# Sliding-window attention beside a gated FFN, forward and backward: the short FFN chunk as one block, U's rows turned from SBUF, and fillers on PE

## The chip, the cores and the metric

The kernel runs on one NeuronCore of a Trainium2 chip. The metric is the device time of one execution in microseconds (us). The engines are named as in the profile: PE (TensorE, with PEld for its weight loads), DVE (VectorE), ACT (ScalarE), POOL (GpSimd) and SP (SyncE), which here only issues transfers. "Queue" means the order of an engine's instructions, which is fixed when the program is built.

## The reference

Inputs are x (2048 x 512), the attention weights wqkv and wo, the FFN weights W_gate, W_up (512 x 1376) and W_down (1376 x 512), a gate vector and grad_out, all bf16. Computed are the output and the gradients of x and of all weights (eight tensors):

```python
def _A_ref(x, wqkv, wo):                       # 32 heads of 16, window of 256 keys
    q, k, v = ...                              # x @ wqkv, split into heads
    scores = jnp.einsum("bhqd,bhkd->bhqk", q, k) * (Dh ** -0.5)
    scores = jnp.where(mask, scores, -1e9)     # 0 <= query - key < 256
    return heads_joined(softmax(scores) @ v) @ wo

def _B_ref(x, W_gate, W_up, W_down):           # 1376 columns: ten chunks of 128 and one of 96
    gate = x @ W_gate
    return ((gate * (gate > 0)) * (x @ W_up)) @ W_down

g = sigmoid((x * gate_w).sum(-1, keepdims=True))
out = g * _A_ref(x, ...) + (1 - g) * _B_ref(x, ...)
# and the vector-Jacobian product of out with grad_out
```

## The kernel before

**A planner fixes the order.** The kernel describes its work as operations with costs in ns, ranks, and the buffers that they read and write (`Flow.op`, L210). `Flow.run` (L257) then plays the work through on a model of the five engines, one event after another, and emits each instruction at the moment at which the model starts it. On an engine it takes the ready operation of the lowest rank, and among equal ranks the one described first. A transfer on SP has a cost for its issue (430 ns, 1300 ns for a turning one, if nothing else is given) and a model of the DMA engines for its end. So the costs, ranks and buffer counts set the order of every queue; the chip then runs those queues as they are. PE work is of three modes ("row" for scores, "col" for sums over keys, "den" for dense 128 x 128 matmuls), and a change of mode costs 98 ns in the model. The eight PSUM banks are shared by kinds of work, each with a cap (`bank`).

**The stages.** First, to some 55 us, the inputs are loaded, turned to column form, and the first quarter of the projections is made. Then attention runs over 32 stages (`NS`; eight groups of four heads times four blocks of 512 rows, one U per stage). Its "row" operations have rank 0; all dense work has higher ranks and fills what PE has left: projections of the other head groups (`proj`, rank 3.5, L715), `front(fc)` of the FFN chunks (rank 4, L803), `back(fc)` (rank 4, L850), the weight gradients `dw(c)` of attention (4.05 to 4.7, L1190) and the FFN products for the first twelve row tiles (`early`, 4.6). After attention, from about 730 us, come the last row tiles, `final` and `whole`, and dw(3).

**The FFN around the change.** `front(fc)` makes, for each of four blocks of 512 rows, three products (L828) of a chunk's 128 columns, and stores them to DRAM as `ffn_d[fc, w, p, s]` (L830). Chunk 10 has only 96 columns (`fsz`). `back(fc)` needs the same data with rows in the partitions: `load_acts` turns them with DMA transposes, one per block for a full chunk (L840, three products at once, 384 rows) and three per block for the short one (L845, 96 rows each). `back` then makes 16 matmuls into each of five banks (L855 on, by way of `accumulate`, whose matmuls are recorded at L622) and stores three results. The loop over chunks (L1102) goes 0 to 10, `back` three chunks behind `front` (`LAG`), and the last three `back`s stand at the end. `group(g)` (L1238) reads the FFN products of all chunks again (L1245, L1248, L1253) for the dense products that are recorded at L1300; its transfers depend on all of `ffn_d`, so none can start before the last chunk is stored.

**U.** In each stage `tasks_A1` (L1021) computes U (128 x 512), which DVE and POOL use. The key-side sums (`tasks_N`, matmuls at L1012) need U with rows in the partitions, R. U is stored to DRAM (`U_d[n]`, L1049) and read back by a DMA transpose (L1050). U has one buffer, R three.

**Other lines in the numbers.** L944: row matmuls; L986: exponentials on ACT; L992: DVE products of attention; L962: masks on POOL; L889 to L891: loads of a stage; L1070 and L1093: stores of attention's results `HD_d`; L1194: turns of `HD_d` for dw; L1276: loads of `HD_d` for the tail.

Of the kernel before, what the change touches and what calls it, by code (L numbers as in the profile page):

```python
# [44 lines left out]
PE, DVE, ACTE, POOL, SP = "PE", "DVE", "ACT", "POOL", "SP"  # L45
LATENCY = {PE: 230, DVE: 130, ACTE: 150, POOL: 100, SP: 2300}
SWITCH = 98
BACKLOG = 1500
HOLD, WAIT = 2.5, 800

# [148 lines left out]
class Flow:  # L199
# [7 lines left out]
    def __init__(self):  # L207
        self.ops = []
# [48 lines left out]
    def run(self):  # L257
# [4 lines left out]
        self.log = []  # L262
# [6 lines left out]
        def offer(o):  # L269
            o.at = now  # L270
            for e in o.times:
                ready[e].append(o)

# [9 lines left out]
        while done < len(self.ops):  # L283
            progress = True
            while progress:
                progress = False
                for e in (PE, ACTE, DVE, POOL, SP):
# [3 lines left out]
                    if dma_free > now + BACKLOG:  # L291
                        cands = [o for o in cands if o.rank < 3 or not o.nbytes]
                    if not cands:
                        continue
# [12 lines left out]
                    if e == PE:  # L307
                        if o.mode != mode:
                            took += SWITCH
                        mode = o.mode  # L310
                        if o.mode == "den":
                            heavy = o.heavy
# [20 lines left out]
            while events and events[0][0] <= now:  # L333
                _, _, what, o = heapq.heappop(events)
                if what == "done":
                    done += 1
                    o.state = 2
                    if not o.lead:
                        for b in o.uses:
                            b.drop()  # L340
                    release(o.after)
                elif what == "lead":
                    for b in o.uses:
                        b.drop()
# [3 lines left out]
def kernel(  # L348
# [61 lines left out]
    ffn_d = Buf(None, dram.tile([FC, 3, P, S], BF, name="ffn_d"))  # L410
    U_d = [Buf(None, dram.tile([P, W], BF, name=f"U_d{n}")) for n in range(NS)]
# [391 lines left out]
    def front(fc):  # L803
        fs = fsz(fc)
        wg, wu, wdT = wsets.pop(("f", fc))
        for tg in range(NSB):
# [20 lines left out]
            for k, (a, b) in enumerate((("rg", "upm"), ("dhs", "upm"), ("dhs", "rg"))):  # L827
                op({POOL: t_pool(W, 2), DVE: DTT}, lambda e, q=q, k=k, a=a, b=b: EN[e].tensor_tensor(  # L828
                    out=q["act"][:fs, k, :], in0=q[a][:fs, :], in1=q[b][:fs, :], op=ALU.mult), r=[q[a], q[b]], w=[(q["act"], k)], rank=3)
            dma(lambda q=q, sl=sl: nc.sync.dma_start(ffn_d[fc, :, :fs, sl].rearrange("w p s -> p w s"), q["act"][:fs]), r=[q["act"]],  # L830
                w=[(ffn_d, (fc, tg))], nbytes=384 * KB, rank=2)

    def load_acts(fc):
        fs = fsz(fc)
        rows = []
        for tg in range(NSB):
            sl = slice(tg * W, (tg + 1) * W)
            rw = buf("rows")
            if fs == P:
                dma(lambda rw=rw, sl=sl: nc.sync.dma_start_transpose(  # L840
                    out=rw[:].rearrange("p k w f -> p k (w f)"), in_=ffn_d[fc, :, :, sl].rearrange("w p s -> (w p) s")),
                    r=[(ffn_d, (fc, tg))], w=[rw], nbytes=384 * KB, rank=2, turn=True, ns=1500)
            else:
                for w in range(3):
                    dma(lambda rw=rw, sl=sl, w=w: nc.sync.dma_start_transpose(out=rw[:, :, w, :fs], in_=ffn_d[fc, w, :fs, sl]),  # L845
                        r=[(ffn_d, (fc, tg))], w=[rw], nbytes=100 * KB, rank=2, turn=True)
            rows.append(rw)
        return rows

    def back(fc):  # L850
        rows = load_acts(fc)
        fs, f0 = fsz(fc), fc * P
        wst, dst = buf("wst"), buf("dst")
        for c in range(DC):
            bank = buf("mm")  # L855
            accumulate(bank, [mm(lambda bank=bank: bank[:, 0:2 * fs], lambda t=t, c=c: x_r[:, t, c * P:(c + 1) * P],
                                 lambda t=t: rows[t // 4][:, t % 4, 1:3, :fs]) for t in range(NT)], rows + [x_r], BACK, [wst],
                       cols=2 * fs, step=8)
            op(either(2 * P), lambda e, bank=bank, c=c: copy(e, wst[:, c, :, :fs],
                                                             bank[:, 0:2 * fs].rearrange("p (a f) -> p a f", a=2)),  # L860
               r=[bank], w=[wst], rank=2)
# [4 lines left out]
        accumulate(bank, [mm(lambda: bank[:fs, :D], lambda t=t: rows[t // 4][:, t % 4, 0, :fs], lambda t=t: db_r[:, t, :])  # L866
# [154 lines left out]
    def tasks_A1(n, us):  # L1021
# [10 lines left out]
        def b1(segs):  # L1032
# [16 lines left out]
        dma(lambda: nc.sync.dma_start(U_d[n][:], U[:]), r=[U], w=[U_d[n]], nbytes=128 * KB, rank=1)  # L1049
        dma(lambda: nc.sync.dma_start_transpose(out=R[:], in_=U_d[n][:]), r=[U_d[n]],  # L1050
            w=[R], nbytes=128 * KB, rank=1, turn=True)
# [50 lines left out]
    for fc in range(FC):  # L1102
        if fc:
            load_ffn(fc)
        front(fc)
        if fc >= LAG:
            back(fc - LAG)
    for fc in range(FC - LAG, FC):
# [129 lines left out]
    def group(g):  # L1238
# [3 lines left out]
        for f in range(0, FC, 4):  # L1242
# [4 lines left out]
            if f + 4 > NF:  # L1247
                dma(lambda gh=gh, hi=hi, f=f: nc.sync.dma_start(gh[:fl_, hi - f, :], ffn_d[hi, 0, 0:fl_, gsl]), r=[ffn_d], w=[gh],  # L1248
                    nbytes=48 * KB, rank=3.1)
            hs.append(gh)  # L1250
        for f in range(FC):
            gd = buf("gd")
            dma(lambda gd=gd, f=f: nc.sync.dma_start(gd[:fsz(f)], ffn_d[f, 1:3, :fsz(f), gsl].rearrange("w p s -> p w s")),  # L1253
                r=[ffn_d], w=[gd], nbytes=128 * KB, rank=3.1, row=512)
# [198 lines left out]
    with tc.manual_schedule(engines={eng.PE, eng.Activation, eng.DVE, eng.Pool, eng.SP}):  # L1453
        fl.run()
# [27 lines left out]
```

## Time and profile before

| | before |
|---|---|
| three runs | 849.79, 860.8, 861.84 us |
| median | 860.8 us |
| profiled execution: span, first to last instruction | 853.1 us |
| profiled execution: its own end-to-end time | not listed; the median is 7.7 us above its span |
| mean granted TensorE clock | 0.984 |
| PE busy | 810.4 us (95%) |
| DVE busy | 707.9 us (83%) |
| ACT busy | 598.6 us (70%) |
| POOL busy | 526.6 us (62%) |
| DMA packets, bytes | 317818, 156.38 MB |

The profile is of one execution. Its page has busy times, the span in 40 slices of 21.3 us (each digit a tenth of busy time, or of the granted clock), DMA queues, the chain of waits that ended last, and the costliest groups of instructions. Asked for stretches, it gives for each engine busy us and, in parentheses, the number of instructions, then the granted PE clock, the DMA share and GB/s. Matmuls are pipelined and their records overlap, so a busy PE is not PE at its peak. SP's rows (SPq) are issues: their length is the time that the issue held the queue, not that of the transfer.

### The profile page before, as it was taken

The numbers are of one execution on the slowest core, as the hardware profiler recorded it, in microseconds if no ns is written. First come the engines' busy times: TensorE is split into PE (matmuls) and PEld (weight loads), VectorE is DVE, ScalarE is ACT, GpSimd is POOL, SyncE is SP. The second block draws the span as 40 slices with busy tenths as digits, with TensorE's granted clock in tenths as the row PEclk, the third lists the DMA queues.
The fourth block names the chain that finished last, engine by engine and source line by source line (L and its number), as shares of the span: only waits on it lengthen the run. The fifth ranks groups of instructions, "written<-read, shape, count | busy, mean of one in ns | idle before, by whom it ended". The sixth has DMA issues, their size and how long they took to land.

```text
span 853.1 us, 24192 instructions
## 1 busy us (share of the span) xinstructions
PE 810.4 (95%) x8834; PEld 388.9 (46%) x8952; DVE 707.9 (83%) x1312; ACT 598.6 (70%) x1212; POOL 526.6 (62%) x928
## 2 busy tenths in 40 slices
PE   8999999999999999999999989899999999899996
PEld 5534533535354544544545445443333435343444
DVE  3579899999999999998999998898999899614333
ACT  4778888888888778777888878888887787100113
POOL 5469778676697887777987755656665655002111
PEclk9999999999999999999999969999999999899999
DMA  7989656465699999899555367968655643768793
GB/s 204 230 179 224 165 147 184 119 149 142 135 239 226 214 219 218 238 206 207 152 132 117 90 159 184 279 157 242 197 174 152 179 150 101 220 186 281 214 221 99
DMA packets 317818, 156.38 MB, mean 183 GB/s; under 512 B 202817, under 2 KB 310402, under 8 KB 316930
## 3 DMA queue, kind: packets, MB, share of 16 engines
q1 hardware_dynamic: 302522, 141.78, 66.7%
q10 hardware_dynamic: 14600, 11.47, 4.5%
q0 software_dynamic: 576, 1.57, 1.0%
q8 instruction: 70, 1.15, 0.6%
q14 instruction: 50, 0.41, 0.2%
HBM read 55.02 MB, written 59.93 MB: 135 GB/s over the span
## 4 chain that ended last, share of the span: by engine, by line
PE 48%; DMA 10%; DVE 5%; issue 3%; ACT 2%; POOL 1%; SPq 1%; ACTq 1%; DVEq 0%; POOLq 0%
PE banks L622 16%; PE banks L1300 11%; PE banks L944 9%; DMA arena<-HD_d 7%; PE banks L1012 6%; DVE arena L992 3%; PE banks L1215 3%; PE banks L1213 2%; ACT arena L986 1%; DMA arena<-ffn_d 1%; SPq L1194 1%; PE banks L1045 1%; DMA arena<-QD_d_1_119 1%; DMA arena<-U_d_76 1%; DMA arena<-dx_p_145 1%
## 5 line engine op out<-in xcount | busy, mean ns | idle before, releaser
L992 DVE TENSOR_TENSOR arena<-arena,banks 128x512 bf16<-128x512 bf16 (+2 forms) x768 | 460.0, 646 | 33.5 <-PE banks L944 19.9
L986 ACT ACTIVATE arena<-banks 128x512 bf16<-128x512 f32 (+2 forms) x768 | 398.5, 573 | 81.5 <-PE banks L944 72.3
L962 POOL TENSOR_SCALAR_AFFINE_SELECT arena<-arena 128x256 bf16<-128x256 bf16 (+1 forms) x736 | 350.3, 499 | 168.0 <-ACT arena L986 150.3
L622 PE MATMUL banks<-arena 128*128 128x512 bf16 (+3 forms) x1648 | 333.9, 335 | 9.6 <-issue 2.9
L622 PEld LDWEIGHTS <-arena 128*128 128x128 bf16 (+1 forms) x1728 | 151.6, 99 | 138.3 <-issue 55.9
L1300 PE MATMUL banks<-arena 128*128 128x512 bf16 (+1 forms) x747 | 184.2, 384 | 5.4 <-issue 2.1
L944 PE MATMUL banks<-arena 32*128 32x384 bf16 (+2 forms) x2816 | 165.6, 278 | 10.1 <-DVE arena L992 3.0
L944 PEld LDWEIGHTS <-arena 32*128 32x128 bf16 x2816 | 51.2, 92 | 149.6 <-issue 137.1
L600 ACT CAST arena<-banks 128x512 bf16<-128x512 f32 (+4 forms) x173 | 84.1, 497 | 47.4 <-PE banks L622 24.4
L1300 PEld LDWEIGHTS <-arena 128*128 128x128 bf16 (+1 forms) x784 | 70.0, 98 | 94.9 <-issue 21.5
L828 POOL TENSOR_TENSOR arena<-arena 128x512 bf16<-128x512 bf16 (+1 forms) x87 | 102.0, 1174 | 16.8 <-DVE arena L823 11.3
L1012 PE MATMUL banks<-arena 128*32 128x384 bf16 (+5 forms) x2816 | 103.6, 280 | 4.3 <-DVE arena L992 1.6
L1012 PEld LDWEIGHTS <-arena 128*32 128x32 bf16 (+1 forms) x2816 | 58.8, 95 | 42.3 <-issue 25.2
L1397 POOL TENSOR_TENSOR arena<-arena 128x512 f32<-128x512 f32 x12 | 15.2, 1266 | 100.0 <-DMA arena<-dx_p_143 45.6
L1213 PE MATMUL banks<-arena 128*128 128x128 bf16 x256 | 45.5, 221 | 3.3 <-DMA arena<-HD_d 3.1
L1041 POOL TENSOR_TENSOR arena<-arena 128x512 bf16<-128x512 f32 x32 | 37.3, 1166 | 17.7 <-ACT arena L1038 8.6
L1396 ACT ACTIVATE arena<-gw_b,arena 128x512 f32<-128x512 bf16 x12 | 8.5, 719 | 56.4 <-DMA arena<-HD_d 27.2
L1215 PE MATMUL banks<-arena 128*128 128x256 bf16 x256 | 47.7, 274 | 0.0
L828 DVE TENSOR_TENSOR arena<-arena 128x512 bf16<-128x512 bf16 (+1 forms) x45 | 31.7, 716 | 3.1 <-ACT arena L600 1.7
L823 DVE SCALAR_TENSOR_TENSOR arena<-arena,banks 128x512 bf16<-128x512 bf16 (+1 forms) x44 | 29.9, 680 | 2.8 <-PE banks L622 1.8
L1213 PEld LDWEIGHTS <-arena 128*128 128x128 bf16 x256 | 24.3, 98 | 9.3 <-issue 8.6
L1215 PEld LDWEIGHTS <-arena 128*128 128x128 bf16 x256 | 25.2, 98 | 6.8 <-issue 3.4
(91 smaller groups left out, 482.3 us busy)
## 6 DMA issues: line engine op xcount, KB each, us to landing
ffn_d<-arena SPq DMA_DIRECT2D x40, 384.0 KB
arena<-ffn_d SPq DMA_DIRECT2D x88, 128.0 KB
out_dram<-arena SPq DMA_DIRECT2D x66, 128.0 KB
HD_d<-arena SPq DMA_DIRECT2D x64, 128.0 KB
arena<-ffn_d SPq DMA_DIRECT2D x16, 256.0 KB
arena<-HD_d ACTq DMA_DIRECT2D x24, 128.0 KB
arena<-HD_d ACTq DMA_DIRECT2D x35, 64.0 KB
arena<-HD_d SPq DMA_DIRECT2D x29, 64.0 KB
```

Source lines behind the costliest of these rows:

```text
L600: nc.scalar.copy(out, in_)
L622: return lambda start, stop: nc.tensor.matmul(out_fn(), lhsT=lhs_fn(), rhs=rhs_fn(), start=start, stop=stop)
L828: op({POOL: t_pool(W, 2), DVE: DTT}, lambda e, q=q, k=k, a=a, b=b: EN[e].tensor_tensor(out=q["act"][:fs, k, :], in0=q[a][:fs, :], in1=q[b] ...
L944: nc.tensor.matmul(bank, lhsT=lt[rs, ls], rhs=rt[rs, rsl], start=True, stop=True)
L962: nc.gpsimd.affine_select(out=v.rearrange("p h (b k) -> p h b k", b=cnt), in_=v.rearrange("p h (b k) -> p h b k", b=cnt), compare_op=ALU.i ...
L986: op({ACTE: t_act(w)}, lambda e, h=h: nc.scalar.activation(nxt.Pt[:, h, :w], nxt.S[h][:, :w], ACT.Exp), r=[nxt.S[h]], w=[(nxt.Pt, h)], rank=0)
L992: op({DVE: t_dve(wc)}, lambda e, h=h: nc.vector.tensor_tensor(out=cur.Pd[:, h, :wc], in0=cur.Pt[:, h, :wc], in1=cur.dP[h][:, :wc], op=ALU. ...
L1012: nc.tensor.matmul(acc[32 * i:32 * i + wt.shape[1], q0:q0 + cnt * P], lhsT=wt, rhs=m[:, i % 2, col * P:(col + cnt) * P], start=(k == 0), s ...
L1041: op({POOL: t_pool(W, 2), DVE: t_dve(W)}, lambda e: EN[e].tensor_tensor(out=U[:], in0=ri[:], in1=qd[:], op=ALU.mult), r=[ri, qd], w=[U], r ...
L1213: nc.tensor.matmul(bank[:, 0:P].rearrange("p (g d) -> p g d", d=Dh), lhsT=x_r[:, t, cd * P:(cd + 1) * P], rhs=RW[:, t, 0:2 * P].rearrange( ...
L1215: nc.tensor.matmul(bank[:, P:3 * P], lhsT=x_r[:, t, cd * P:(cd + 1) * P], rhs=RW[:, t, 2 * P:4 * P], start=False, stop=stop, skip_group_ch ...
L1300: nc.tensor.matmul(bank[:], lhsT=l_(), rhs=r_(), start=(lo + k == 0), stop=(lo + k == n - 1))
```

## The change

Five edits go together:

1. The short chunk's products go to a tensor of their own, `ffn_l`, of 3 x 96 rows in one block, and each block of 512 rows is turned by one transfer of 288 rows, so that the short chunk takes 4 turning transfers, not 12. In the turned buffer its three products stand side by side (96 columns each) instead of 128 apart, and `back` reads them there (`row_of`). The readers of the products in `group` follow.
2. The chunks are worked in the order 0, 1, 2, 3, 4, 10, 5, 6, 7, 8, 9.
3. U is no longer stored to DRAM: the DMA transpose reads it from SBUF.
4. Fillers: when the planner has nothing that PE could start, after 20 us of its time, with a PSUM bank free and fewer than 3600 cycles of PE work in its last 3413 ns, it emits a matmul of the identity with 512 columns of x into the free bank, whose result nobody reads. The bank returns to the free ones when the model has the filler done.
5. The planner's model of PE has a clock: windows of 3413.3 ns, and in a window after one with fewer than 3000 cycles of work, PE's operations take twice their cost. Each PE operation of a rank between 3.4 and 4.3 gets a random 0 to 0.02 added to its rank, from a fixed seed.

```diff
+START = 20000
+SEED = 6
+SPAN, LOW, NEED, PHASE = 3413.3, 3000, 3600, 0
...
+        def lately():
+            return sum(b - max(a, now - SPAN) for a, b in self.busy[-40:] if b > now - SPAN) * 2.4
+
+        def ahead(start, took):
+            w, scale = int((start + PHASE) // SPAN), 1
+            if w not in self.slow:
+                self.slow[w] = ran.get(w - 1, 0) < LOW
+            scale = 2 if self.slow[w] else 1
...
+            return took * scale
...
+        rnd = random.Random(SEED)
+        for o in self.ops:
+            if PE in o.times and o.mode != "row" and 3.4 < o.rank < 4.3:
+                o.rank += rnd.uniform(0, 0.02)
...
+                    if e == PE and not cands and self.spare and self.spare.free and lately() < NEED and now > START:
+                        bank = self.spare.free.pop(0)
+                        took = ahead(now + SWITCH * (mode != "den"), 213) + SWITCH * (mode != "den")
+                        mode = "den"
+                        self.fill(bank)
...
                     if e == PE:
+                        took = ahead(now + SWITCH * (o.mode != mode), took)
...
-    ffn_d = Buf(None, dram.tile([FC, 3, P, S], BF, name="ffn_d"))
-    U_d = [Buf(None, dram.tile([P, W], BF, name=f"U_d{n}")) for n in range(NS)]
+    ffn_d = Buf(None, dram.tile([NF, 3, P, S], BF, name="ffn_d"))
+    ffn_l = Buf(None, dram.tile([3 * (F - NF * P), S], BF, name="ffn_l"))
...
-                for w in range(3):
-                    dma(lambda rw=rw, sl=sl, w=w: nc.sync.dma_start_transpose(out=rw[:, :, w, :fs], in_=ffn_d[fc, w, :fs, sl]),
-                        r=[(ffn_d, (fc, tg))], w=[rw], nbytes=100 * KB, rank=2, turn=True)
+                dma(lambda rw=rw, sl=sl: nc.sync.dma_start_transpose(
+                    out=rw[:].rearrange("p k w f -> p k (w f)")[:, :, :3 * fs], in_=ffn_l[:, sl]),
+                    r=[(ffn_l, tg)], w=[rw], nbytes=288 * KB, rank=2, turn=True, ns=1400)
...
+        def row_of(t, lo, hi):
+            return rows[t // 4][:, t % 4].rearrange("p w f -> p (w f)")[:, lo * fs:hi * fs]
...
-        dma(lambda: nc.sync.dma_start(U_d[n][:], U[:]), r=[U], w=[U_d[n]], nbytes=128 * KB, rank=1)
-        dma(lambda: nc.sync.dma_start_transpose(out=R[:], in_=U_d[n][:]), r=[U_d[n]],
-            w=[R], nbytes=128 * KB, rank=1, turn=True)
+        dma(lambda: nc.sync.dma_start_transpose(out=R[:], in_=U[:]), r=[U], w=[R], nbytes=128 * KB, rank=1, turn=True)
...
-    for fc in range(FC):
+    chunks = list(range(5)) + [NF] + list(range(5, NF))
+    for j, fc in enumerate(chunks):
         if fc:
             load_ffn(fc)
         front(fc)
-        if fc >= LAG:
-            back(fc - LAG)
-    for fc in range(FC - LAG, FC):
+        if j >= LAG:
+            back(chunks[j - LAG])
+    for fc in chunks[FC - LAG:]:
         back(fc)
...
+        fl.spare = psum
+        fl.fill = lambda b: nc.tensor.matmul(banks[:, b * W:(b + 1) * W], lhsT=ident[:], rhs=x_r[:, 0, :], start=True, stop=True)
         fl.run()
```

## The prediction

> **What bounds the kernel now.** I read the page's totals first, then busy time by stretch, then the narrow stretches in which the granted clock drops, then the timelines of PE and SyncE around them, then the chain of waits.
>
> ```profile
> span 853.1 us, 24192 instructions
> PE 810.4 (95%) x8834; PEld 388.9 (46%) x8952; DVE 707.9 (83%) x1312; ACT 598.6 (70%) x1212; POOL 526.6 (62%) x928
> PEclk9999999999999999999999969999999999899999
> ```
>
> The PE row is nearly full, but its records overlap in a pipelined engine, so 95% is not yet a bound. The clock row has two dips, at slice 24 and at slice 35. By stretch:
>
> ```profile
> core 0: us, PE busy (x) PEld busy (x) DVE busy (x) ACT busy (x) POOL busy (x), PEclk, DMA share, GB/s
> 55.00:490.00 435.00, 421.38 (x5034) 204.24 (x5105) 412.81 (x726) 356.84 (x715) 343.52 (x578) 1.00 0.76 177
> 490.00:510.00 20.00, 17.79 (x168) 7.63 (x169) 18.66 (x41) 14.18 (x31) 12.07 (x25) 0.66 0.64 161
> 510.00:730.00 220.00, 212.54 (x2648) 97.08 (x2676) 200.47 (x368) 174.10 (x359) 128.46 (x260) 0.99 0.65 180
> 730.00:853.00 123.00, 109.15 (x583) 52.15 (x590) 46.11 (x118) 18.70 (x41) 15.19 (x12) 0.97 0.74 206
> ```
>
> Attention (55 to 730) has two near-full engines: DVE 412.81 + 18.66 + 200.47 = 631.9 of 675 us (94%) and PE. What DVE leaves idle there, 43 us, is the most that better timing can give while its work stays. After 730 DVE is at 37% and PE at 89%: the tail is PE with transfers in between. The hand-over from FFN to the later dense work lies at 490:
>
> ```profile
> 490.00:495.00 5.00, 4.83 (x50) 2.04 (x50) 5.00 (x14) 4.81 (x11) 4.19 (x10) 0.67 0.58 142
> 495.00:500.00 5.00, 3.30 (x44) 1.21 (x40) 5.00 (x13) 4.70 (x12) 3.19 (x7) 0.50 0.39 106
> 500.00:505.00 5.00, 4.67 (x35) 1.54 (x36) 5.00 (x10) 2.35 (x5) 2.67 (x5) 0.50 0.59 152
> 735.00:740.00 5.00, 4.78 (x15) 1.59 (x12) 1.50 (x2) 0.00 (x0) 0.00 (x0) 0.50 0.75 220
> 491.27 0.51 SPq L830 DMA_DIRECT2D ffn_d<-arena  x1
> 491.83 2.50 SPq L845 DMA_TRANSPOSE arena<-ffn_d  x2
> ...
> 496.37 4.72 SPq L845 DMA_TRANSPOSE arena<-ffn_d  x3
> 499.96 0.58 PE L944 MATMUL banks<-arena 32*128 32x256 bf16 x5 [1.68 <-DVE arena L992]
> 501.96 1.49 PE L622 MATMUL banks<-arena 128*128 128x512 bf16 x3 [0.33 <-issue]
> ```
>
> The reader is to see: the short chunk's last store goes out at 491.27, its turns (L845) hold SyncE until 501.1, and PE has no dense matmul (L622) from 487.8 to 501.96. The clock is granted at half meanwhile, and DVE is full all the same. Lastly the places where the chain of waits runs through U's round trip to DRAM:
>
> ```profile
> 354.50 1.95 DMA U_d_72<-arena
> ...
> 445.56 4.67 DMA arena<-U_d_76
> ...
> 535.00 3.38 DMA arena<-U_d_80
> ...
> PE banks L1012 <- DMA arena<-U_d_80: 1.4, 1, 1.4
> PE banks L1012 <- DMA arena<-U_d_76: 0.4, 1, 0.4
> ```
>
> **The base of the sum.** The profiled execution has a span of 853.1 us; its own end-to-end time is not listed. The three runs are 849.79, 860.8 and 861.84; one is shorter than this span, so the profiled execution is like the two longer ones. I take 860.8 - 853.1 = 7.7 us as what lies around the span and sum against 860.8, the median.
>
> **U's rows turned from SBUF.** Removed: 32 stores (L1049, some 0.43 us of SyncE each, 13.7 us) and their landing. The turn stays one instruction (L1050, 1.2 us, 40.9 us in all). Today its issue follows the store's by 4.6 us in the median stage (1.7 to 7.8, from the starts of the two lines), partly behind other issues. SyncE's rows add up to 550 us of 853 (455 of 675 in attention), so the issue time saved lies beside other work except near 490, where SyncE is 90% issued. What can reach the end is R landing some 4 us sooner: at least PE's own 1.8 us of waits, at most the chain's 1.95 + 4.67 + 3.38 = 10.0 us. I take 5, since DVE loses 2.05 of 5 us in 535 to 540 as well. U has one buffer; it is now held until the turn has read it, not the store, so the next U (one per 21 us stage) is not near that limit. No transfer of before turns out of SBUF, so its price is unknown. The nearest rows are DRAM turns: 1.2 us for 128 x 512, up to 5.04 us (L1194, four times the bytes, at 808). At 5.04, SyncE would issue 32 x (5.04 - 1.28 - 0.43) = 107 us more, within its 220 idle us in attention, but each R would come about as late as today: no gain. I take 1.3, the row of the same shape.
>
> **The short chunk: one block, sixth in order.** Twelve turns (15.7 us of SyncE) become four. A full chunk's four (L840) take 1.57 us each in the median, so four of 288 rows cost about 6: 9.7 us less. Moved sixth, everything that this chunk issues moves: three weight loads, four stores, four turns and three result stores on SyncE, and on POOL and DVE its products (1.17 and 0.72 us each). Today the sixth chunk's stores go out at 264 to 292 and its turns three chunks later; SyncE is 77% issued there (154.9 of 200 us in 230 to 430) and the DMA share near 1.0. The cover is that fronts and backs of three chunks overlap; if it is gone, it costs this chunk's turns, 6 us. Last comes a full chunk: after its last store one turn of about 1.6 us and a landing, instead of 10.7 us to the first dense matmul; I put this at 5, so dense work resumes 5.7 us sooner. That is the upper end. The lower is set by the pace of attention, counted in DVE products (L992): 22 in 490 to 510 and 21 in 510 to 530 against 23.1 per 20 us, so 3.2 of 23.1, or 2.8 us. I take 3. The contiguous 2 x 96 columns in back() change no row's size and cost nothing: the same 16 matmuls per bank.
>
> **Fillers and the planner's clock.** They go where the planner has nothing for PE and under 3600 of 8192 cycles of recent work. In the trace this fits the half-clock stretches: by (1 - clock) x length x 2 they are 13.6 us at 490 to 510, 3.4 at 539 to 543 and 6.9 at 733 to 741, 23.9 in all. If all of PE's lost cycles counted, that is 12 us. The lower bound is what the tail alone shows: 15 long matmuls in 735 to 740 against 24 in a full stretch, 9 x 0.21 = 1.9 us. The runs themselves spread by 12.05 us, which is the size of the upper end, so I take 9, nearer to it. A filler costs its 0.21 us in PE's order plus a weight load of 0.1 beside it; PE idles 13.9 us in the tail, which is the cover; without it, 50 fillers would cost 10 us. I take 1 off: clock 8 net.
>
> [...]
>
> **Ranks and order.** The random 0 to 0.02 reorders only first pieces of ranks between 3.4 and 4.3: projections 1 to 3, front() and back(). Projections of the second and third quarter of the heads are stored by 94 and 160, and the second is first loaded at 176, so a swap of the two is hidden; front() is a chain and cannot swap within itself. Bounds: DVE's 43 idle us on one side, and on the other stages like that from 354.5 to 379.3 (24.8 us against 21.3), one or two of which cost 3.5 to 7. Value taken: 0.
>
> Sum: 860.8 - 5 - 3 - 8 = 844.8, so 845. The attention part of it (about 12) fits in DVE's 43.
>
> **The rivals.**
> - The dip stays: 490 to 510 leaves PE 2.2 us idle, room for seven fillers of 0.31 us, and if these do not lift the activity that the clock follows, its term is nil: 860.8 - 8 = 853. For it: long records of waiting matmuls already fill the row. Against: the planner sees rows of 0.3 us where the trace has 26 in 3.62 us, so it sees more room.
> - Hidden anyway: DVE sets the pace and was full through the dip. Only PE's waits for U (1.8) and the tail's 1.9 come back: 857. For it: DVE 5.00 in three rows at half clock. Against: DVE idles 4.3 us in 505 to 530 right after.
> - All ends at once: 10.0 + 5.7 + 12 = 27.7, so 833, with the clock held everywhere. For it: the 849.79 run, with the same program. Against: it needs the upper end three times.
> - Fillers in PE's way: the planner's idle is not PE's idle; in 750 to 830 PE is busy 95%. With 60 fillers at 0.31 us and no gain from the clock: 860.8 - 5 - 3 + 19 = 872; it is slower than before from some 26 fillers on.
> - SBUF turns are dear: SyncE has 220 idle us in attention, or 6.9 per stage; with the 1.71 of today's store and turn, it is full from 8.6 us per turn. At 10 us each: 845 + 32 x 1.4 = 890, and the stall shows as SyncE full and L1012 waiting for R. For it: no row excludes it; against it: no DRAM turn of 128 KB is above 2.2.
>
> [...]
>
> **How the numbers follow.** Forecast (835 to 852, likeliest 845): 0.40. The dip stays (848 to 858): 0.13. Hidden (853 to 866): 0.10. All ends (818 to 838): 0.24. Fillers in the way (862 to 882): 0.07. Dear turns (above 870): 0.06. The range 826 to 868 leaves out about one in ten on each side. Two per cent, about what a measurement of this kernel can tell from no change, is 843.6 and 878: faster has all of the ends case and near half of the forecast, 0.43; slower has the dear turns and a third of the fillers, 0.08; the rest is 0.49.
>
> **What would show it.** U: no store of U, L1050 issued at once at about 1.2 us, no L1012 wait for R. Chunk: four turns of about 1.5 us near 320, and dense matmuls resuming within 5 us of the last FFN store. Clock: PEclk at 9 from slice 1 to the end. Wrong would be: L1050 above 3 us, an unchanged dip, DVE idle in attention not below 43 us, or PE's busy time in the tail growing with the fillers.

## The result, and the profile after

| | before | after |
|---|---|---|
| median of 20 runs | 852.41 us (848.52 to 861.84) | 857.50 us (853.22 to 869.53) |
| ratio to before, 95% interval | | 1.0052 [1.0028, 1.0076] |
| profiled execution | span 853.1 us | 854.56 us, span 852.8 us |
| granted clock, mean | 0.984 | 0.994 |

The forecast was 845, faster by 1.8%; the kernel became slower by 0.5%. The ratio leaves out runs more than 1.5% above the fastest of their kernel (two of the twenty after), so it lies a little below 857.50 / 852.41 = 1.006. The base moved as well: the three runs shown had 860.8 as their median, twenty have 852.41. What lies around the span is 854.56 - 852.8 = 1.8 us in the profile after, not 7.7. The profiled execution of before therefore took about 853.1 + 1.8 = 854.9, and the two profiled executions are equally long. They show what changed inside, not where 0.5% went.

The page after, its totals and the clock by slice:

```profile
span 852.8 us, 24276 instructions
PE 822.9 (96%) x8965; PEld 386.3 (45%) x8965; DVE 711.4 (83%) x1313; ACT 597.9 (70%) x1201; POOL 533.8 (63%) x938
PEclk9999999999999999999999999999999999999999
```

By stretch, with the columns of the table of before:

```profile
core 0: us, PE busy (x) PEld busy (x) DVE busy (x) ACT busy (x) POOL busy (x), PEclk, DMA share, GB/s
55.00:490.00 435.00, 423.40 (x5013) 198.45 (x5012) 412.67 (x718) 349.80 (x698) 347.71 (x581) 1.00 0.73 168
490.00:510.00 20.00, 18.08 (x221) 8.95 (x220) 18.73 (x44) 16.79 (x37) 13.13 (x27) 1.00 0.98 227
510.00:730.00 220.00, 217.89 (x2692) 97.33 (x2691) 203.19 (x374) 175.32 (x354) 129.07 (x262) 1.00 0.64 171
730.00:853.00 123.00, 111.72 (x614) 53.66 (x611) 45.23 (x115) 19.19 (x42) 15.20 (x12) 0.97 0.73 205
```

Both dips are gone from the clock row, and 490 to 510 runs at 1.00 where it ran at 0.66. Half-clock time (without the program's first 20 and last 10 us) fell from 23.9 to 10.2 us. Yet attention, to its last DVE product, ends at 733.6 after and 734.8 before. Of PE's idle time one must be careful: before has 8834 matmul records for 8952 weight loads, after 8965 for 8965. The 118 missing records leave apparent gaps of two sizes in PE's rows: 73 of about 0.053 us and 45 of about 0.155 us, 10.8 us in all, where the trace after has nine gaps of these sizes (1.0 us). So some 10 of the 12.5 us by which PE's busy time grew (810.4 to 822.9) are records, not work. From 55 us to the end of attention, without gaps of these sizes, PE idles 15.2 us before and 14.6 after. Of the prediction's other signs, DVE's idle time in 55 to 730 went from 43.1 to 40.4 us, and PE's busy time in the tail from 109.15 to 111.72.

The rows of SyncE for U's turn and for the short chunk's turn (duration min/median/max in ns, then first and last start in us):

```profile
L1097 SPq DMA_TRANSPOSE arena<-arena x32: 1188/1204/2082, 45.7 to 710.7; - x32
...
L888 SPq DMA_TRANSPOSE arena<-ffn_l x4: 1367/1479/2031, 281.7 to 318.5; - x4
```

Both prices are as forecast: 1.2 us for U's turn out of SBUF (1.3 forecast), 1.48 us for each of four turns (1.5 forecast). PE's longest waits after:

```profile
PE banks L1093 <- DVE arena L1091: 4.7, 5, 2.3
PE banks L1348 <- DMA arena<-wt_d: 3.2, 1, 3.2
PE banks L992 <- DVE arena L1040: 2.4, 6, 0.8
PE banks L1260 <- DMA arena<-HD_d: 2.3, 1, 2.3
```

No wait for U is left. In first place stands L1093, a stage's matmul with `bones`, which needs a result of L1091 on DVE: 4.7 us in five places. Before had 1.8 us of waits for U, and this matmul (its L1045) waited 0.9 us in all. The waits have new places. The hand-over at 490, from the timelines of SyncE and PE:

```profile
490.99 0.38 SPq L871 DMA_DIRECT2D ffn_d<-arena  x1
491.92 1.48 PE L662 MATMUL banks<-arena 128*128 128x512 bf16 x10
...
504.60 5.43 SPq L884 DMA_TRANSPOSE arena<-ffn_d  x3
506.40 1.04 PE L662 MATMUL banks<-arena 128*128 128x512 bf16 x4
...
509.49 0.82 PE L1503 MATMUL banks<-arena,ident 128*128 128x512 bf16 x3
510.71 0.61 PE L1503 MATMUL banks<-arena,ident 128*128 128x512 bf16 x2
512.50 1.04 PE L662 MATMUL banks<-arena 128*128 128x512 bf16 x4
```

Dense work (L662) goes on 0.93 us after the last FFN store, as foreseen. But the full chunk's last turns (L884) now issue 13.6 us after that store, with the DMA share at 0.98 in this stretch against 0.64 before. The gap that is left lies at 509 and holds five of the kernel's fillers. There are few of them in all:

```profile
L1503 PE MATMUL banks<-arena,ident 128*128 128x512 bf16 x13 | 4.1, 420 | 0.0
```

### The profile page after: what moved, and what is told of

The parts are those of the page before. It is cut to its first block, busy times and chain, and to the rows that moved or that the text cites. A ratio compares the mean times of both kernels' runs of the same rounds, so it can differ in the third digit from the quotient of the medians.

```text
span 852.8 us, 24276 instructions
## 1 busy us (share of the span) xinstructions
PE 822.9 (96%) x8965; PEld 386.3 (45%) x8965; DVE 711.4 (83%) x1313; ACT 597.9 (70%) x1201; POOL 533.8 (63%) x938
## 4 chain that ended last, share of the span: by engine, by line
PE 44%; DMA 6%; POOL 6%; DVE 6%; issue 3%; ACT 1%; SPq 1%; ACTq 0%; DVEq 0%; POOLq 0%
PE banks L1348 16%; PE banks L662 11%; PE banks L992 8%; PE banks L1060 5%; DVE arena L1040 3%; POOL arena L868 3%; DMA arena<-HD_d 3%; POOL arena L1010 3%; PE banks L1262 2%; PE banks L1260 2%; DMA arena<-wt_d 1%; SPq L1241 1%; DMA arena<-ffn_d 1%; ACT arena L1034 1%; DMA arena<-in_B_W_down_dram 1%
## 5 line engine op out<-in xcount | busy, mean ns | idle before, releaser
L662 PE MATMUL banks<-arena 128*128 128x512 bf16 (+3 forms) x1728 | 345.8, 337 | 1.4 <-DVE arena L1040 0.8
L662 PEld LDWEIGHTS <-arena 128*128 128x128 bf16 (+1 forms) x1728 | 150.3, 99 | 136.4 <-issue 55.8
L1348 PE MATMUL banks<-arena 128*128 128x512 bf16 (+1 forms) x784 | 190.2, 385 | 3.4 <-DMA arena<-wt_d 3.2
L992 PE MATMUL banks<-arena 32*128 32x384 bf16 (+2 forms) x2816 | 164.4, 276 | 7.2 <-DVE arena L1040 2.4
L992 PEld LDWEIGHTS <-arena 32*128 32x128 bf16 x2816 | 50.4, 92 | 150.2 <-issue 137.2
L868 POOL TENSOR_TENSOR arena<-arena 128x512 bf16<-128x512 bf16 (+1 forms) x92 | 107.8, 1175 | 12.7 <-DVE arena L863 6.9
L1445 POOL TENSOR_TENSOR arena<-arena 128x512 f32<-128x512 f32 x12 | 15.2, 1266 | 100.4 <-DMA arena<-dx_p 51.2
L1060 PEld LDWEIGHTS <-arena 128*32 128x32 bf16 (+1 forms) x2816 | 58.0, 94 | 39.4 <-issue 26.3
L868 DVE TENSOR_TENSOR arena<-arena 128x512 bf16<-128x512 bf16 (+1 forms) x40 | 29.4, 742 | 2.5 <-ACT arena L640 1.8
L1440 DVE SCALAR_TENSOR_TENSOR arena<-banks,g_all,arena 128x512 bf16<-128x512 f32 x12 | 9.0, 749 | 22.9 <-DMA arena<-b_d 22.6
L1260 PEld LDWEIGHTS <-arena 128*128 128x128 bf16 x256 | 24.1, 97 | 8.4 <-issue 7.4
```

Of the source, the lines that this page charges most:

```text
L662: return lambda start, stop: nc.tensor.matmul(out_fn(), lhsT=lhs_fn(), rhs=rhs_fn(), start=start, stop=stop)
L992: nc.tensor.matmul(bank, lhsT=lt[rs, ls], rhs=rt[rs, rsl], start=True, stop=True)
L1060: nc.tensor.matmul(acc[32 * i:32 * i + wt.shape[1], q0:q0 + cnt * P], lhsT=wt, rhs=m[:, i % 2, col * P:(col + cnt) * P], start=(k == 0), s ...
L1260: nc.tensor.matmul(bank[:, 0:P].rearrange("p (g d) -> p g d", d=Dh), lhsT=x_r[:, t, cd * P:(cd + 1) * P], rhs=RW[:, t, 0:2 * P].rearrange( ...
L1348: nc.tensor.matmul(bank[:], lhsT=l_(), rhs=r_(), start=(lo + k == 0), stop=(lo + k == n - 1))
```

## The experiments

Each ratio is to the kernel before on the same chip. The expectations use these names: A, DVE sets the pace of attention; B, the prediction's sum; C, a turn out of SBUF has a hidden price; D, PE sets the pace and each change of its mode costs about 0.1 us, as in the planner (98 ns); E, fillers and the planner's clock cost time; F, longer pieces of dense work hold up the row matmuls. G and H are stated where they first appear. "Old order" means that every queue of before keeps its order. "Dealt anew" means that the planner plans again with the edit, so all queues change.

**U's edit alone, old order.** The planner still plans the store, but it is not issued.

```diff
-        dma(lambda: nc.sync.dma_start(U_d[n][:], U[:]), ...
+        dma(lambda: None, ...
-        dma(lambda: nc.sync.dma_start_transpose(out=R[:], in_=U_d[n][:]), ...
+        dma(lambda: nc.sync.dma_start_transpose(out=R[:], in_=U[:]), ...
```

> The kernel before with U turned from SBUF and its 32 stores left out, every queue's order as before. Theory A (the waits for U lie beside DVE work, which sets the pace of attention): within 2 us of the kernel before, ratio 0.997 to 1.002, with the waits of L1012 for U gone. Theory B (the prediction's: R some 4 us sooner reaches the end): 4 to 6 us less, ratio 0.993 to 0.995. Theory C (a turn out of SBUF has a hidden price, which made the changed kernel slower): 3 us or more slower, ratio above 1.003.

Measured: 1.0003 [0.997, 1.0037]. A gain of 5 us (0.994) is excluded, and so is a hidden price of more than some 3 us. One wait for R stays, as long as its longest before (1.4 us), with the turn now out of SBUF:

```profile
PE banks L1012 <- DMA arena<-arena: 1.4, 1, 1.4
```

**The short chunk as one block, at its old place, old order.** Four turns of 288 rows, each at the third of the planned turns.

```diff
+    ffn_l = Buf(None, dram.tile([3 * (F - NF * P), S], BF, name="ffn_l"))
-                for w in range(3): dma(... in_=ffn_d[fc, w, :fs, sl]) ...
+                for w in range(3): dma(... in_=ffn_l[:, sl]) if w == 2 else None ...
```

> The kernel before with the short chunk stored as one block and turned by 4 transfers, its place (last) and every queue's order as before; the third of the three planned turns carries the block. Theory A (DVE sets the pace): within 2 us, ratio 0.997 to 1.002, though dense matmuls resume 2 to 4 us sooner after the last FFN store. Theory B (the prediction's): 3 us less, ratio 0.996 or below, and a shorter stretch at half clock near 490 to 505.

Measured: 1.0004 [0.9968, 1.0039]. The dip is still there (from 490.4, 10.2 us at half clock). Eight turns fewer are worth nothing that can be measured. Nor did dense work (here L623) resume sooner after the last FFN store, as A expected: the store goes out at 487.73 and dense work comes at 499.11, 11.4 us later, where it was 10.7 before.

```profile
492.05 1.32 SPq L847 DMA_TRANSPOSE arena<-ffn_l  x1
...
497.11 0.58 PE L951 MATMUL banks<-arena 32*128 32x256 bf16 x5 [1.68 <-DVE arena L999]
497.62 1.15 PE L1019 MATMUL banks<-arena 128*32 128x384 bf16 x16
499.11 1.49 PE L623 MATMUL banks<-arena 128*128 128x512 bf16 x3 [0.34 <-issue]
```

The last turn is issued 7 us before dense work, which stands in PE's queue behind matmuls of attention that wait for DVE.

**Less for DVE, old order.** From the third stage on, attention's products of 512 columns are cut to 384.

```diff
+                wd = min(wc, 384) if wsets["cut"] > 2 * 24 else wc
-                    out=cur.Pd[:, h, :wc], in0=cur.Pt[:, h, :wc], ...
+                    out=cur.Pd[:, h, :wd], in0=cur.Pt[:, h, :wd], ...
```

> The kernel before, order kept, with DVE's products of attention computed on 384 of their 512 columns from the third stage on (the rest of Pd is left as it was, so the gradients are not the reference's). This takes 0.13 us off some 590 DVE instructions, 79 us of DVE time. Theory A (DVE sets the pace of attention): attention ends 30 us or more sooner, span 825 or less. Rival (PE sets it): attention ends less than 10 us sooner, span above 843.

Measured: 0.9975 [0.995, 1.0]. Its stretches:

```profile
55.00:490.00 435.00, 423.10 (x5062) 204.56 (x5131) 377.17 (x733) 358.82 (x721) 345.47 (x582) 1.00 0.75 177
490.00:730.00 240.00, 230.40 (x2819) 104.66 (x2848) 193.30 (x408) 185.69 (x384) 137.48 (x278) 0.97 0.66 180
```

```profile
L994 DVE TENSOR_TENSOR arena<-arena,banks x768: 405/547/690, 52.0 to 728.9; 128x384 bf16<-128x384 bf16 x166, 128x256 bf16<-128x256 bf16 x16, 128x512 bf16<-128x512 bf16 x10
```

In 55 to 730 DVE has 570.5 us of work where it had 631.9, 61 us less. Attention ends at 729.4, 5.4 us sooner, and the kernel is 2 us shorter. A full engine that can lose a tenth of its work with so little effect does not set the pace alone. A falls.

**Less for PE, old order.** Every fourth matmul of the sums that `accumulate` makes is left out, so the results of these sums are not the reference's.

```diff
                 for k in range(lo, hi):
-                    mms[k](k == 0, k == len(mms) - 1)
+                    if k % 4 != 2:
+                        mms[k](k == 0, k == len(mms) - 1)
```

> The kernel before, order kept, with every fourth matmul of the dense sums of 4 and 16 left out (projections, FFN, weight gradients; their results are not the reference's). This takes some 70 us of matmul streaming out of PE's queue in attention. Theory A (DVE sets the pace): attention ends less than 10 us sooner. Rival (PE sets it): attention ends 30 us or more sooner. If both this and the run with less DVE work gain 10 to 30, the two engines hold each other up stage by stage.

Measured: 0.9786 [0.9743, 0.9828].

```profile
55.00:490.00 435.00, 393.62 (x4736) 183.14 (x4800) 423.49 (x755) 364.21 (x737) 351.09 (x595) 0.99 0.77 179
```

```profile
L993 DVE TENSOR_TENSOR arena<-arena,banks x768: 404/678/697, 50.9 to 721.1; 128x512 bf16<-128x512 bf16 x160, 128x384 bf16<-128x384 bf16 x16, 128x256 bf16<-128x256 bf16 x16
PE banks L945 <- DVE arena L993: 9.6, 20, 1.7
PE banks L945 <- DVE arena L1048: 6.0, 13, 1.2
```

PE's busy time in this stretch falls by 27.8 us, and DVE rises from 412.81 to 423.49 of 435, with 11.5 us of idle time left. Attention ends at 721.8, 13.0 us sooner. That is neither the 30 us of "PE sets it" nor under the 10 us of A. Much of what was taken from PE came back as its own idle time (in attention, without the gaps of missing records, 15.2 us before and 42.6 here), with more waits of the row matmuls (L945) for DVE. So work taken from PE's queue is worth more than work taken from DVE, but PE does not set the pace alone either: DVE is right behind.

**U's edit alone, dealt anew.** U's edit as in the change, nothing else.

> The kernel before with U turned from SBUF, its store taken out of the planner's work too, so that all queues are dealt again. On PE this makes 893 runs of one mode (row, col, den) where the kernel before has 862 and the changed one 903. Theory D (PE sets the pace, and each change of mode in its queue costs it some 0.1 us): 31 more changes, 2 to 4 us slower, ratio 1.002 to 1.005, though the same edit with the order kept cost nothing. Rival E (fillers and the planner's clock cost the changed kernel its time): same as before, ratio 0.998 to 1.002. Prediction's step (R sooner): 4 to 6 us faster.

Measured: 1.0123 [1.0079, 1.0167]. The same edit that was worth nothing costs 10 us once the queues are dealt anew; its turns take 1216 ns in the median, so C falls here too. The ratio lies above what D and E expected. Attention ends at 742.4.

**U's edit in dense pieces of four.** `accumulate` and `group` offer dense matmuls in pieces of four instead of two, which leaves fewer changes of mode (807 runs of one mode in PE's queue against 862).

```diff
-    def accumulate(bank, mms, r, rank, keep=(), cols=512, step=2, ...
+    def accumulate(bank, mms, r, rank, keep=(), cols=512, step=4, ...
-        for lo in range(0, n, 2): part = pairs[lo:lo + 2]
+        for lo in range(0, n, 4): part = pairs[lo:lo + 4]
```

> U turned from SBUF with its store still planned, and dense sums dealt in pieces of 4 matmuls instead of 2: 807 runs of one mode on PE instead of 862. Theory D: 55 fewer changes of mode, 4 to 7 us faster, ratio 0.992 to 0.996. Rival F (longer pieces hold up the row matmuls that attention waits for): slower, ratio above 1.003.

Measured: 1.0241 [1.0192, 1.029], the highest ratio of all, with the fewest changes. D falls as an account of the time. The last stretches of its attention, which ends at 760.0:

```profile
685.00:715.00 30.00, 24.70 (x304) 10.32 (x303) 26.86 (x51) 24.66 (x50) 20.35 (x45) 0.63 0.25 66
715.00:760.00 45.00, 34.96 (x407) 14.65 (x406) 42.48 (x74) 26.95 (x58) 22.13 (x45) 0.54 0.35 74
```

Here the dense work that can lie beside attention is used up before attention ends (no matmul of L622 or L1300 from 685 to 760), the clock is granted at 0.54 to 0.63, and attention ends at that pace. That the run is slower is as F has it, but longer pieces are not shown to be the cause.

**The short chunk alone, dealt anew.** The changed kernel with U's store planned but not issued, without fillers, planner's clock and random ranks: one block, sixth place, and U turned from SBUF, which was worth nothing in the old order.

> The changed kernel with the planner as before (no fillers, no clock in it, no random ranks) and U's store still planned but not emitted: what is left is the short chunk as one block, sixth in order, and U turned from SBUF. 827 runs of one mode on PE. Theory D: 35 fewer than before, 2 to 5 us faster, ratio 0.994 to 0.998. Rival: the chunk's new place does not count, ratio 0.998 to 1.002.

Measured: 1.0099 [1.007, 1.0129]; attention ends at 747.7, and half-clock time is 41.0 us. Both expectations miss: D had it faster, its rival equal.

**The changed kernel with its 13 fillers not issued**, its order kept.

> The changed kernel with its order kept and its 13 fillers planned but not emitted. Theory D: within 1.5 us of the changed kernel, so still above the kernel before, ratio 1.002 to 1.007. Rival E (fillers stand in PE's way): the loss is gone, ratio 0.998 to 1.002. Prediction's step (fillers hold the clock): slower than the changed kernel, ratio above 1.008, with half-clock stretches back near 244, 509 and 740.

Measured: 1.0026 [0.999, 1.0062]. The interval overlaps that of the change (1.0052 [1.0028, 1.0076]). Half-clock time doubles to 20.5 us, and no loss shows: the prediction's fillers would have needed a ratio above 1.008. E is not excluded, since the interval holds both its range (0.998 to 1.002) and D's (1.002 to 1.007).

**Random ranks alone.** So far all deals were slower than the old one. Is it the edits, or the dealing? Four runs, the first on the kernel before, the others on the changed kernel.

```diff
+        rnd = random.Random(6)
+        for o in self.ops:
+            if PE in o.times and o.mode != "row" and 3.4 < o.rank < 4.3:
+                o.rank += rnd.uniform(0, 0.02)
```

> The kernel before with one thing of the change alone: the random 0 to 0.02 on ranks 3.4 to 4.3, with its seed 6; no other edit, so the same instructions are dealt in another order. The runs so far leave two readings of why each edit is worth nothing in the old order and each re-dealt order is slower (1.0123, 1.0241, 1.0099, 1.0026). Theory G (any new deal of PE's queue is some tenths of a per cent to one per cent worse than the order that the kernel before happens to have): ratio 1.003 to 1.015, attention ending at 737 to 748 and not at 734.8. Rival H (it is the edits that make the planner deal worse, by turning U sooner and by the short chunk in sixth place, and an idle shuffle of dense work does nothing): ratio within 0.997 to 1.003 and attention ending within 2 us of 734.8.

> The changed kernel without the random part of the ranks (the planner plans 39 fillers in place of 13). Theory G: the seed of the changed kernel is one draw, and the deal without it is another, so the ratio lies anywhere from 1.00 to 1.015, most likely above the 1.0052 of the changed kernel, about 1.010. Rival H: as the changed kernel, 1.003 to 1.007.

> The changed kernel with seed 1 for the random ranks in place of 6 (21 fillers). Theory G: another draw, 1.00 to 1.015, about 1.010, and differing from the run with seed 3 by more than 0.3%. Rival H: as the changed kernel, 1.003 to 1.007.

> The changed kernel with seed 3 for the random ranks in place of 6 (25 fillers). Theory G: another draw, 1.00 to 1.015, about 1.010, and differing from the run with seed 1 by more than 0.3%. Rival H: as the changed kernel, 1.003 to 1.007.

Measured: 1.0212 [1.0165, 1.0258] for the kernel before with random ranks; for the changed kernel 1.0199 [1.0158, 1.024] without them, 1.001 [0.9981, 1.004] with seed 1 and 1.0127 [1.0084, 1.0169] with seed 3. H falls, and G's sign holds, but G was too mild: the shuffle costs 2.1%, above its range of 0.3 to 1.5%, and the changed kernel without random ranks lies above its 1.5% too. The last product of attention (the fields after the durations are the first and last start) in before, then in before with random ranks:

```profile
L992 DVE TENSOR_TENSOR arena<-arena,banks x768: 401/678/690, 53.1 to 734.1; 128x512 bf16<-128x512 bf16 x160, 128x384 bf16<-128x384 bf16 x16, 128x256 bf16<-128x256 bf16 x16
```

```profile
L997 DVE TENSOR_TENSOR arena<-arena,banks x768: 402/676/690, 53.1 to 754.4; 128x512 bf16<-128x512 bf16 x160, 128x384 bf16<-128x384 bf16 x16, 128x256 bf16<-128x256 bf16 x16
```

The same 768 products of the same length end 20.3 us later. Half-clock time grows from 23.9 to 37.5 us, worth 7 us at most, and PE's longest waits there are these (its L997 is L992 of before, L1048 is L1043), followed by that of before:

```profile
PE banks L1050 <- DVE arena L1048: 6.8, 3, 6.2
PE banks L949 <- DVE arena L997: 6.7, 11, 2.6
```

```profile
PE banks L944 <- DVE arena L992: 3.0, 3, 1.7
```

From 55 us to the end of attention, without the gaps of missing records, PE idles 15.2 us in before and 25.6 here, and half of the half-clock time, the most that it can cost, goes from 8.9 to 15.4 us. Together that is 16.9 of the 20.3 us, as an estimate; the rest is not resolved. The shuffle reaches beyond the operations that it touches: SyncE's operations get no random rank, and its issues come in another order from 82 us on.

**Fillers alone, old order.** PE's queue of before with 87 fillers put in, wherever the planner left PE idle for 0.21 us or more from 480 to 740 us of its time; then the same with U's edit and the block.

```diff
                     if e == PE:
+                        n = int((now - self.pe_end) / 213) if 480000 <= now < 740000 and self.spare.free else 0
+                        for j in range(n):
+                            self.fill(self.spare.free[j % len(self.spare.free)])
```

> The kernel before, with fillers of 512 columns put into PE's queue between 480 and 740 us of the planner's time wherever it leaves PE idle for 0.21 us or more before an operation of its (87 fillers); every other instruction keeps its place on its queue. The prediction's clock step: the dips at 490, at 535 and at 734 go, and with the whole of attention's half-clock time back this gives up to half of its about 18 us, so 843 to 849, ratio 0.988 to 0.994. The prediction's rival (hidden anyway): the clock is 1.00 in the dips, but DVE and the chain of each stage were full through them; ratio 0.997 to 1.003. Rival (fillers in PE's way): 87 fillers at 0.21 to 0.31 us are 18 to 27 us, of which what is not idle on the chip is paid; 1.005 to 1.02.

> All the edits that leave the old order alone, in one kernel: U turned from SBUF and its store not emitted, the short chunk stored as one block and turned by four transfers at its old place, and the 87 fillers of the run with fillers alone. If the parts are worth nothing each and do not meet: the same ratio as that run within 0.4%. By the prediction's sum (5 + 2.8 + half-clock time): 0.978 to 0.985.

Measured: 1.0118 [1.0079, 1.0158] and 1.0098 [1.0063, 1.0132]. Of the first, stretches and the fillers' row (busy us, mean ns, then idle us before them and what ended it):

```profile
490.00:510.00 20.00, 16.93 (x182) 7.66 (x178) 16.37 (x37) 13.60 (x28) 10.01 (x20) 1.00 0.58 144
510.00:730.00 220.00, 211.65 (x2595) 95.29 (x2625) 196.25 (x357) 173.00 (x356) 127.95 (x258) 0.99 0.65 178
```

```profile
L1461 PE MATMUL banks<-arena,ident 128*128 128x512 bf16 x80 | 23.5, 394 | 10.7 <-ACT arena L992 4.6 <-DVE arena L998 4.0 <-ACT arena L606 0.9
```

(Its L992 is L986 of before, the exponentials, and its L998 the DVE products, L992.) The dip's clock is 1.00, and half-clock time falls from 23.9 to 6.8 us. All the same DVE does less there (16.37 against 18.66 us, 37 against 41 instructions), and attention ends 6.3 us later, at 741.1. A filler needs a bank. The planner holds it for free, but on the chip ACT or DVE is still reading it, and the filler waits, with the row matmuls queued behind it: 10.7 us of waits and 23.5 us of work. This is the prediction's rival "Fillers in PE's way" in kind, at about half its price: 87 fillers cost 10 us here, where the rival had 19 us for 60. That its total (872, +11) is near is chance, since it holds a gain of 8 us for U and the short chunk that is not there. What the clock alone brings is not separated here from what the fillers cost. The two runs agree within 0.2%, so U's edit and the block bring nothing in company either.

**Two more deals of the kernel before, random ranks only.**

> The kernel before with random ranks only, seed 1 in place of 6 (no other edit). Theory G (the old order was a good deal, and the edits on average do not hurt): 1.005 to 1.025, above the mean of the changed kernel's four deals, 1.010. Rival (the edits do hurt and seed 6 was a poor deal): 0.998 to 1.005.

> The kernel before with random ranks only, seed 3. Theory G: 1.005 to 1.025. Rival (the edits do hurt and seed 6 was a poor deal): 0.998 to 1.005.

Measured: 1.0207 [1.0171, 1.0243] and 1.0235 [1.0196, 1.0274], as G has it. Attention ends at 753.5 and 753.3, 18.7 and 18.5 us later than in before. Counted as above, PE's idle time there (21.7 and 26.3 us) and half of the half-clock time (19.2 and 18.9 us) make 16.8 and 21.1 us more than before. So in all three shuffles the loss is about as large as PE's added waiting and its lower clock together.

**The change without planner's clock and fillers**, with seeds 6 and 1: U, the short chunk in sixth place, random ranks.

> The changed kernel without fillers and without the planner's clock: U from SBUF, the short chunk as one block in sixth place, random ranks with seed 6. If U and the short chunk bring the gain over jittered deals of the kernel before (mean 1.0218): about 1.005, as the changed kernel. If the planner's clock and fillers bring it: about 1.020.

> The same with seed 1. If U and the short chunk bring the gain: 1.000 to 1.010. If the planner's clock and fillers bring it: about 1.020. One near 1.005 and one near 1.020 would leave it open.

Measured: 1.0108 [1.0072, 1.0144] and 1.0089 [1.0055, 1.0123]: the first between the two answers, the second inside the range of "U and the short chunk". With random ranks in all of them:

| seed | before | + U and short chunk | + clock and fillers (the change) |
|---|---|---|---|
| 6 | 1.0212 | 1.0108 | 1.0052 |
| 1 | 1.0207 | 1.0089 | 1.001 |
| 3 | 1.0235 | not run | 1.0127 |
| half-clock us, seed 6 / seed 1 | 37.5 / 44.4 | 30.7 / 41.0 | 10.2 / 13.7 |

Against a deal with random ranks, U and the short chunk bring 1.0 and 1.2% (9 and 10 us), with intervals that do not meet, and the planner's clock with its fillers 0.6 and 0.8% (5 and 7 us; for seed 6 the intervals just meet). Without random ranks it is otherwise: U 1.0123, the short chunk with U 1.0099, all but the random ranks 1.0199. So these differences hold between deals and cannot be read as prices of the edits. A seed is also not the same shuffle in two programs, since the operations that it meets differ.

## Why the prediction was wrong, step by step

- **The step that failed: "Ranks and order", value 0.** Any new deal of the queues was slower than or equal to the old: twelve of them lie from 1.001 to 1.0241. The random ranks alone cost the kernel before 2.07 to 2.35%, some 18 to 20 us, and the prediction bounded them by 3.5 to 7. It asked only what the random part can swap by itself (a few first pieces). It did not ask that each swap moves bank, buffer and transfer times in the planner, and by them later choices: with random ranks, SyncE's order too differs from 82 us on. And it put the edits' effects on dealing at nothing although all five pass through the planner.
- **"U's rows turned from SBUF", -5.** The price of a turn was right (1.3 taken, 1.2 measured), and in the changed kernel the store and PE's waits for R are gone, as forecast. The term was wrong: nothing in the old order, where 1.4 us of waits for R stayed. R was hardly ever late (1.8 us of waits before), and the chain's 10 us were not time that PE could take back. The rival "SBUF turns are dear" falls: the median turn takes 1.204 us.
- **"The short chunk", -3.** Four turns of 1.48 us where 1.5 was forecast, dense work going on at once, no dip. At its old place the block is worth nothing. The gap of 10.7 us was laid to the turns, but the prediction's own line at 501.96 shows 0.33 us of "issue" before the first dense matmul and no wait for a transfer: until then PE's queue was given over to attention's matmuls. In sixth place the block could only be had with a new deal.
- **"Fillers and the planner's clock", -8.** The clock was repaired as forecast (23.9 to 10.2 us at half), and only 13 fillers were needed. That a repair by fillers is worth 8 us fell: in the old order the dip goes and the kernel is 1.2% slower, and the changed kernel without its fillers is not measurably slower. The planned idle time of PE was not PE's idle time.
- **The cover, "DVE's 43 idle us".** DVE was taken for the pace of attention. A tenth less of DVE work in attention changes 0.25%; 6% less of PE's work changes 2.1%. PE's queue, in its order, bound more than DVE, with DVE right behind it. A near-full engine was mistaken for the limit.
- **The base.** 7.7 us around the span was 1.8. The median of three was 8.4 us above that of twenty, so the forecast of -16 us from 860.8 is best read as a ratio, 0.982.
- **The clock and PE's gaps.** In before the clock fell to 0.50 at 491.7 with PE's longest gaps at 1.06 us (to 489.94) and, inside the dip, 1.68 us (to 499.96). In the changed kernel a single gap of 2.35 us ends at 243.65, and the clock is at half from 243.5 to 246.9; with 87 fillers in the old order, 490 to 510 keeps 1.00. Which measure of PE's work the clock follows is not shown, and no run tests the limits of the planner's clock.

**How the end came out.** For seed 6 the sums go from 852.4 by +18.1 (random ranks), -8.9 (U and short chunk) and -4.8 (clock and fillers) to 856.8, the change's own ratio times 852.4, so the sum is no check of its parts. It is one path of several; by the path without random ranks, all the other edits cost 2.0% and the random ranks gain 1.5%. That 857.5 lies in the ranges of two rivals, "The dip stays" (848 to 858) and "Hidden anyway" (853 to 866), is chance: the dip went, and DVE did not set the pace.

**What stays open.** What makes one deal 2% better than another is not settled. The count of mode changes does not order them (before 862, its slower random deals 856, 832 and 862, the change 903). Half-clock time does not either: 23.9 us in before, and as much in the changed kernel without random ranks, which is 2% slower. Nor do PE's idle time and the clock together cover every deal: with U's edit dealt anew they make 0.7 us less than before, and attention ends 7.6 us later. Most of the loss of the slower deals lies in attention: it ends at 734.8 in before and between 737.9 and 760.0 in the other deals (at 733.6 in the profiled execution of the change, one of its shorter ones), while the tail behind it takes 113 to 123 us in all (118.3 in before; 4.8 more in two of the deals, U's edit dealt anew and seed 1 of U and the short chunk). Whether the sixth place has a worth of its own was not separated from the new deal that it forces.

## What to carry to other kernels

Where a planner deals the queues, an edit is tried first with the old order kept (the removed step planned but not issued); that shows its price without a new deal, though not a gain that needs another order, and a few seeds with and without it show whether a difference is more than the deal. An engine that is 94% busy is tested by taking work from it before its idle time is used as a bound. Idle slots of the plan were not idle slots of the chip: the 87 fillers put there waited 10.7 us, mostly for banks that the plan believed free, and attention ended 6.3 us later.

## What the runs showed of the hardware

- A DMA transpose of 128 x 512 from SBUF held SyncE as long as one from DRAM: 1204 ns against 1212 ns in the median of 32 turns. One of 288 rows took 1479 ns, one of 384 rows 1547 ns in the median: three times the rows, 1.3 times the issue.
- Stretches at half clock were 13.65, 3.41 and 6.83 us long in before (from 491.7, 539.5 and 734.0) and three times 3.41 us in the changed kernel (from 243.5, 745.2 and 789.6). The half-clock times given above for the other runs (6.8 to 44.4 us) are whole multiples of 3.41 us as well.
- In the changed kernel PE's gaps of 2.35 us (to 243.65) and 2.24 us (to 789.80) each came with one such piece. A gap of 2.31 us there (to 834.47) and one of 2.63 us in before (to 834.74) did not: the clock reads 1.00 from 830 to 840 in both.
- With the granted clock lifted from 0.66 to 1.00 over 20 us by fillers in the old order, attention ended 6.3 us later, the fillers' cost included.
- PE's records overlap: in before, 880 matmuls of 128x512 on L622 last 383 ns in the mean, 337 us added up, within 235.0 us of busy time.
- The trace of before lacks 118 of 8952 matmul records, while its weight loads are all there. They leave apparent idle gaps of about 0.053 us (73 of them) and 0.155 us (45), so PE's idle times of two kernels can be compared only after the records are counted against the weight loads.
